# First MLP of a fused attention and two-MLP kernel: one visit of four units per token tile and group, later tile's h kept in the attention's buffers

## Chip, cores and metric

One core of a Trainium2 (trn2) chip. The metric is the device time of one execution in microseconds (us), as the median of several runs.

## What is computed

A block-summary attention (2 batches, 8 heads, 768 positions, head dimension 64), then two MLPs over its 1536 tokens of 512 channels, both with 2048 hidden units. The first MLP's activation is a rational function, the second's is h cos(h). All data are float32, the weights of the MLPs float64.

```python
def _attn_ref(q, k, v):
    block, window = (32, 16)
    k_sum = k.reshape(B, H, nb, block, D).max(axis=3)
    v_sum = v.reshape(B, H, nb, block, D).mean(axis=3)
    scores_l = scale * np.matmul(q, k.transpose(0, 1, 3, 2))
    scores_s = scale * np.einsum('bhsd,bhnd->bhsn', q, k_sum) + np.log(block)
    # softmax over |i - j| < 16 and the 24 block summaries, times v and v_sum

def _moe_ref(x, w_in, w_out, a, b):
    h = x @ w_in
    P = a[0] + a[1] * h + a[2] * h2 + a[3] * h3
    Q = 1.0 + np.abs(b[0]) * np.abs(h) + np.abs(b[1]) * h2
    return (P / (Q + 1e-06)) @ w_out

def _moe2_ref(x, w_in, w_out):
    h = x @ w_in
    return (h * np.cos(h)) @ w_out
```

## The kernel before

The instructions of all engines are recorded first by Python functions as operations with their reads and writes (`P.op`, where "T" is TensorE, "A" ScalarE, "V" VectorE, "P" GpSimd and "S" SyncE, whose queue issues the DMAs). A table of numbers, `ORDER`, then gives the sequence in which the operations are issued, and for each the engine where several are allowed (`Plan.order`). So the order on an engine isn't the order of the code.

*Attention.* Twelve query tiles u of 128 tokens. `attn_a` (L605 on) gathers the windows of k, multiplies q by them (tiles `sp`, L633), adds the mask and takes the minimum on VectorE (L663), the exponential with its row sum on ScalarE (L667), adds 1e-9 to the row sums (L672, L674), takes the reciprocal (L677) and scales (L680), the last three once for each of the two halves `hh` of the heads. `attn_b` transposes (L694), `attn_c` multiplies by v (`avp`, L741) and writes x transposed in two parts, high and low (`xH`, `xL`), since every product is done as three float32r matmuls: high by high, high by low, low by high. A query tile also needs the k tiles and the means of v (`k_pair`, `k_tile`, `v_mean0`, `v_mean1`).

*MLPs.* The tokens are three tiles T of 512. The hidden units are 16 slices f of 128, in four groups of four (`G = 4`). A unit is a pair (T, f): `mlp_h` (L909) makes h in a PSUM bank from 12 matmuls, the activation (`ew1` or, for Strassen pairs, `ew1s`) makes g and splits it into `gh` and `gl`, and `mlp_o` (L1307) multiplies g by the output weights into four PSUM accumulators, acc0 to acc3 (12 matmuls, L1341). The outputs of a unit come three units after its h (`LA = 3`). The accumulators hold one token tile at a time. A stretch of consecutive units of one T is called a visit here. At its end the accumulators are copied out to a partial sum in SBUF (`part` for T = 0 and 1, `room` for T = 2), or, after the last slice, kept as the next MLP's x (`x_keep`). At the start of a later visit they are copied back into PSUM (the `if un.first and have` branch of `mlp_o`). All of these copies are 128 x 512, on ScalarE or VectorE.

In the first group tile 0 is done in two halves of 256 columns (c = 0 and 256), so that it can begin when two of its four query tiles are done. In the later groups tiles 0 and 1 are a Strassen pair: `mlp_h4` (L1087) makes the h of two slices f, f + 1 and both tiles by seven products of six matmuls (L1111) instead of eight. Its parts h11, h12, h21, h22 are copied out of, or added to, three PSUM banks (`keep`, `plus`, L1119 to L1124) into four tiles of the pool `t`, where they wait for their activation. `sum_pair` (L819) makes the four sums of weights that the products need (S1 to S4, high and low), for every second pair in a buffer of tag `big`, for the others in four buffers that the attention has left (tags `sc`, `sc`, `pt`, `qk`). `x_pair0` makes the sums of x. `conv` converts weights from float64 (three VectorE instructions, L767, L771, L775) and splits them (L784); `run_conv` says when.

The order of units in a later group, before: tile 2 stands alone, first or last; tile 1 is entered with two slices, then tile 0 with four, then tile 1 with two.

```python
    two = [(1, f0), (1, f0 + 1)] + [(0, f0 + i) for i in range(G)] + [(1, f0 + 2), (1, f0 + 3)]
    flat += [(T, f, 0, TT) for T, f in (single + two if g % 2 else two + single)]
```

In the second MLP tile 2 has a Strassen form of its own (`mlp_h2`, L1160) and its visits are as in the first. `mlp_end` (L1378) finishes the last accumulator of the last unit in two halves of 256 columns, each with its own copy and transfer.

## Times and profile before

| | us |
|---|---|
| median of 3 runs | 595.98 (595.64 to 599.79) |
| the profiled execution | 596.73 |
| its span, first to last instruction | 595.0 |
| TensorE matmul busy | 574.7 (97%) |
| VectorE busy | 540.3 (91%) |
| ScalarE busy | 449.2 (75%) |
| GpSimd busy | 351.8 (59%) |

PE is the matmul side of TensorE, PEld its weight loads, DVE VectorE, ACT ScalarE, POOL GpSimd, SPq SyncE's queue. A group of rows names the line of the kernel, the engine, the operation and its tiles as out<-in. "Idle before" is the time for which the engine had nothing to do just ahead of an instruction, with what ended it. PEclk is the granted TensorE clock as a share of full speed. Matmuls overlap in their pipeline: one of 512 columns takes some 390 ns, and the next begins 227 ns after it.

### The profile page before, as it was taken

To read this page: it belongs to the slowest core of one execution; us is meant where nothing else is said; L and a number is where in the kernel's file an instruction comes from. 1 tells how busy PE (TensorE), PEld (TensorE's weight loads), DVE (VectorE), ACT (ScalarE), POOL (GpSimd) and SP (SyncE) were. 2 spreads that over 40 slices of the span, in tenths; PEclk is the share of its full clock that TensorE was granted. 3 is DMA by queue.
4 is the path that set the end of the run, shared out by engine and by line. 5 is a ranking of instruction groups with operands and counts; after the bars stand their busy time and mean duration, and the time that the engine had idled before them with its cause. 6 is when DMAs were issued, how large, how long until landed. Compare 5 with 4: busy or idle time off the path is not lost.

```text
span 595.0 us, 10350 instructions
## 1 busy us (share of the span) xinstructions
PE 574.7 (97%) x3567; PEld 477.0 (80%) x3567; DVE 540.3 (91%) x1101; ACT 449.2 (75%) x980; POOL 351.8 (59%) x342
## 2 busy tenths in 40 slices
PE   7969999999999999999999899999999999999997
PEld 6568787888888787888778678888889888888886
DVE  4999999999999999999899999998997898897773
ACT  3989999989799999999799996856446234555452
POOL 5768978767879677777777606354444415344031
PEclk9999999999999999999999999999999999999999
DMA  8996941301122131312122221113322132020013
GB/s 243 284 257 168 254 100 42 98 21 56 67 73 69 37 106 36 105 51 93 36 71 72 72 72 36 43 64 106 107 71 72 36 103 75 1 72 0 2 72 141
DMA packets 68861, 51.83 MB, mean 87 GB/s; under 512 B 37304, under 2 KB 63160, under 8 KB 68808
## 3 DMA queue, kind: packets, MB, share of 16 engines
q1 hardware_dynamic: 68664, 51.03, 29.1%
q8 instruction: 28, 0.46, 0.3%
q14 instruction: 25, 0.20, 0.1%
q10 hardware_dynamic: 144, 0.13, 0.1%
HBM read 47.71 MB, written 3.15 MB: 85 GB/s over the span
## 4 chain that ended last, share of the span: by engine, by line
PE 56%; ACT 21%; DVE 15%; issue 3%; POOL 2%; DMA 2%; SPq 1%; DVEq 0%; ACTq 0%; POOLq 0%
PE acc L1341 26%; PE h L1111 12%; PE h L924 7%; PE h L1160 6%; ACT acc L328 2%; ACT tt L1211 2%; ACT h L1215 2%; ACT h L1229 2%; DVE f L775 1%; PE ptp L694 1%; ACT gh L328 1%; ACT tf L1213 1%; PE avp L741 1%; ACT part L328 1%; DVE sc L663 1%
## 5 line engine op out<-in xcount | busy, mean ns | idle before, releaser
L1341 PE MATMUL acc<-gh,w 128*128 128x512 f32 (+1 forms) x416 | 123.3, 379 | 2.7 <-ACT acc L328 2.7
L1341 PE MATMUL acc<-w,gh 128*128 128x512 f32 x382 | 118.1, 391 | 0.0
L784 POOL TENSOR_TENSOR gl<-tt,gh 128x512 fp32r<-128x512 f32 (+1 forms) x59 | 75.6, 1284 | 53.1 <-ACT gh L328 34.5
L1341 PEld LDWEIGHTS acc<-gh,w 128*128 128x128 f32 x416 | 75.2, 188 | 19.0 <-ACT acc L328 4.8
L1341 PEld LDWEIGHTS acc<-w,gh 128*128 128x128 f32 x382 | 70.5, 188 | 14.0 <-ACT part L322 0.4
L784 POOL TENSOR_TENSOR w<-f,w 128x512 fp32r<-128x512 f32 x44 | 60.1, 1369 | 30.8 <-DVE w L333 23.3
L1341 PE MATMUL acc<-gl,w 128*128 128x512 f32 (+1 forms) x208 | 77.7, 373 | 0.0
L1341 PE MATMUL acc<-w,gl 128*128 128x512 f32 x191 | 74.4, 390 | 0.0
L328 ACT COPY tt<-h 128x512 f32<-128x512 f32 (+1 forms) x66 | 35.2, 538 | 30.3 <-PE h L1111 19.3
L924 PE MATMUL h<-big,w 128*128 128x512 f32 x216 | 53.0, 389 | 0.0
L1298 ACT ACTIVATE h<-h 128x512 f32<-128x512 f32 x48 | 27.3, 579 | 30.0 <-DVE h L1295 29.8
L924 PEld LDWEIGHTS h<-big,w 128*128 128x128 f32 x216 | 40.5, 188 | 8.5
L1292 ACT ACTIVATE h<-tt 128x512 int32<-128x512 f32 x48 | 28.6, 602 | 24.6 <-DVE tt L1124 8.6
L771 DVE SCALAR_TENSOR_TENSOR f<-raw,f 128x512 int32<-128x512 int32 x64 | 46.5, 729 | 0.4
L775 DVE SCALAR_TENSOR_TENSOR f<-raw,f 128x512 int32<-128x512 int32 x64 | 46.1, 728 | 0.3
L1341 PEld LDWEIGHTS acc<-gl,w 128*128 128x128 f32 x208 | 39.1, 188 | 7.0
L1295 DVE SCALAR_TENSOR_TENSOR h<-h,tt 128x512 f32<-128x512 int32 x48 | 32.9, 694 | 10.3 <-ACT h L1292 10.2
L1341 PEld LDWEIGHTS acc<-w,gl 128*128 128x128 f32 x191 | 35.9, 188 | 7.6
L1111 PE MATMUL h<-xH,w 128*128 128x512 f32 x120 | 41.7, 390 | 0.0
L328 ACT COPY part<-acc 128x512 f32<-128x512 f32 x50 | 29.0, 591 | 12.7 <-PE acc L1341 12.6
L1220 POOL TENSOR_TENSOR tt<-tt,tf 128x512 f32<-128x512 f32 x21 | 29.3, 1396 | 15.4 <-ACT tt L1211 10.5
L667 ACT ACTIVATE sc<-sc,mn 128x120 f32<-128x120 f32 x96 | 37.3, 392 | 0.0
(267 smaller groups left out, 1593.0 us busy)
## 6 DMA issues: line engine op xcount, KB each, us to landing
raw<-in_moe_w_in_dram SPq DMA_DIRECT2D x32, 512.0 KB, 4.1
raw<-in_moe_w_out_dram SPq DMA_DIRECT2D x32, 512.0 KB, 3.4
vw<-in_v_dram SPq DMA_DIRECT2D x24, 192.0 KB, 4.0
qk<-in_q_dram SPq DMA_DIRECT2D x10, 256.0 KB, 4.3
out_dram<-part SPq DMA_DIRECT2D x8, 256.0 KB, 2.4
part<-in_k_dram SPq DMA_DIRECT2D x8, 192.0 KB, 6.0
big<-in_v_dram SPq DMA_DIRECT2D x3, 512.0 KB, 6.8
qk<-in_k_dram SPq DMA_DIRECT2D x6, 256.0 KB, 4.8
```

The lines of the kernel that those rows point to most:

```text
L328: nc.scalar.copy(out=o, in_=i)
L667: lambda e, pr=pr, hh=hh, sv=sv: nc.scalar.activation(out=sv()[:, pr, :], in_=sv()[:, pr, :], func=ACTF.Exp, scale=-1.0, bias=mn.t[:, hh, ...
L771: lambda e: nc.vector.scalar_tensor_tensor(out=ft.t.bitcast(I32), in0=lohi()[1], scalar=-0x40000000, in1=ft.t.bitcast(I32), op0=ALU.bitwis ...
L775: lambda e: nc.vector.scalar_tensor_tensor(out=ft.t.bitcast(I32), in0=lohi()[0], scalar=29, in1=ft.t.bitcast(I32), op0=ALU.logical_shift_r ...
L784: lambda e: E[e].tensor_tensor(out=lo(), in0=x(), in1=hi().bitcast(F32), op=ALU.subtract),
L924: nc.tensor.matmul(out=h.t[:, 0:n], lhsT=lt, rhs=rt[:, kk, cs], start=(k0 == 0 and i == 0), stop=(k0 == 2 and i == 5))
L1111: nc.tensor.matmul(out=bank.t, lhsT=lt, rhs=rt, start=start and i == 0, stop=stop and i == 5, skip_group_check=True)
L1160: nc.tensor.matmul(out=bank.t[:, c], lhsT=lt, rhs=rt, start=start and i == 0, stop=stop and i == 5, skip_group_check=True)
L1220: lambda e: E[e].tensor_tensor(out=U(), in0=U(), in1=Z(), op=ALU.add))
L1292: lambda e: nc.scalar.activation(out=H().bitcast(I32), in_=S_(), func=ACTF.Identity, scale=1.0 / PER, bias=0.25))
L1295: lambda e: nc.vector.scalar_tensor_tensor(out=H(), in0=H().bitcast(I32), scalar=-PER, in1=S_(), op0=ALU.mult, op1=ALU.add))
L1341: nc.tensor.matmul(out=dst, lhsT=lt, rhs=rt, start=(un.start and not have and i == 0), stop=(un.stop and i == 2), skip_group_check=have)
```

## The change

- The first group does only slices 0 and 1 of tile 0 in halves; slices 2 and 3 are whole.
- In each later group of the first MLP tiles 0 and 1 are visited once each, with four units, tile 0 first in odd groups and tile 1 first in even ones. So tile 1 of group 1 is followed by tile 1 of group 2 without a break.
- `mlp_h4` keeps the two h tiles of the later tile of each pair in the attention's buffers (`sc`, `sc` for the first pair of a group, `pt`, `qk` for the second).
- `sum_pair` therefore puts all its sums into the `big` buffer, the two pairs of a group in its two halves, and `run_conv` holds back a pair's conversion until the pair four slices earlier has been multiplied (`made4`).
- In the attention, from query tile 2 on, the two halves' row sums get one add and one reciprocal together.
- `mlp_end` does the last accumulator's matmuls in whole width; the copies and transfers stay halves.
- `ORDER` is another table. The matmuls' `start` flags follow the new units.

```diff
--- before.py
+++ after.py
@@ -54,54 +54,53 @@
 
 
 ORDER = (
-    "c-rk)OOGVSagL14dcWV@UEN*%n0`#ZXNEJgyED79yIhjH;*ydnT9gQ
...
+    "c-rk*OOG5!a*mA1toOUBtGcSIr(e@O(=*K(a%RMbNQsXnceRu#P~=h
...
 )
 
 
@@ -667,20 +666,23 @@
                      lambda e, pr=pr, hh=hh, sv=sv: nc.scalar.activation(
                          out=sv()[:, pr, :], in_=sv()[:, pr, :], func=ACTF.Exp, scale=-1.0,
                          bias=mn.t[:, hh, pr:pr + 1], accum_out=su.t[:, hh, pr:pr + 1]))
-            sus = [su[hh, pr] for pr in range(NP)]
+            scs.append((sv, [sc[pr] for pr in range(NP)]))
+        for hs in ([0], [1]) if u < 2 else ([0, 1],):
+            sus = [su[hh, pr] for hh in hs for pr in range(NP)]
+            sl = slice(hs[0], hs[-1] + 1)
             P.op([("A", 0.11), ("V", Shared(0.08))], [], sus,
-                 lambda e, hh=hh: (nc.scalar.activation(out=su.t[:, hh], in_=su.t[:, hh],
+                 lambda e, sl=sl: (nc.scalar.activation(out=su.t[:, sl], in_=su.t[:, sl],
                                                         func=ACTF.Identity, bias=1e-9) if e == "A" else
-                                   nc.vector.tensor_scalar(out=su.t[:, hh], in0=su.t[:, hh], scalar1=1e-9,
+                                   nc.vector.tensor_scalar(out=su.t[:, sl], in0=su.t[:, sl], scalar1=1e-9,
                                                            scalar2=None, op0=ALU.add)))
             P.op([("V", 0.09)], [], sus,
-                 lambda e, hh=hh: nc.vector.reciprocal(out=su.t[:, hh], in_=su.t[:, hh]))
-            ss = [sc[pr] for pr in range(NP)]
-            P.op([("P", Shared(0.95)), ("V", dve2(480))], sus, ss,
+                 lambda e, sl=sl: nc.vector.reciprocal(out=su.t[:, sl], in_=su.t[:, sl]))
+        for hh in range(2):
+            sv, ss = scs[hh]
+            P.op([("P", Shared(0.95)), ("V", dve2(480))], [su[hh, pr] for pr in range(NP)], ss,
                  lambda e, hh=hh, sv=sv: E[e].tensor_tensor(
                      out=sv(), in0=sv(), in1=su.t[:, hh].unsqueeze(2).to_broadcast([128, NP, KW]),
                      op=ALU.mult))
-            scs.append((sv, ss))
         pr_t[u] = scs
         P.now += SPT
 
@@ -827,16 +829,10 @@
                   lambda w=w: w.t[:, 1, :], prio)
             made0[f + i] = w
             ws.append(w)
-        if f % 4 == 0:
-            if not spare2:
-                spare2.append(new("big", [128, 8, 512], F32R, "big", 2))
-            bt = spare2[0]
-            four = [(bt[i], lambda i=i: bt.t[:, i]) for i in range(f % 8, f % 8 + 4)]
-        else:
-            four = []
-            for tag, nb in (("sc", 4), ("sc", 4), ("pt", 3), ("qk", 3)):
-                r = new("qk" if tag == "qk" else "at", [128, 512], F32R, tag, nb)
-                four.append((r, lambda r=r: r.t))
+        if not spare2:
+            spare2.append(new("big", [128, 8, 512], F32R, "big", 2))
+        bt = spare2[0]
+        four = [(bt[i], lambda i=i: bt.t[:, i]) for i in range(2 * f % 8, 2 * f % 8 + 4)]
         A, B = slice(0, 256), slice(256, 512)
 
         def add(o, i0, i1, op, reads, writes):
@@ -1093,7 +1089,11 @@
         for i in range(2):
             for T in range(2):
                 un = u[i, T]
-                un.s = tmp("te")
+                if l == 0 and T != first:
+                    pn, tag, nb = (("at", "sc", 4), ("at", "sc", 4), ("at", "pt", 3), ("qk", "qk", 3))[f % 4 + i]
+                    un.s = new(pn, [128, 512], F32, tag, nb)
+                else:
+                    un.s = tmp("te")
                 un.s2 = [un.s]
                 un.h = (bc if T else bb) if i == 0 or T != first else ba
                 un.hb = [un.h]
@@ -1341,7 +1341,7 @@
                     nc.tensor.matmul(out=dst, lhsT=lt, rhs=rt,
                                      start=(un.start and not have and i == 0),
                                      stop=(un.stop and i == 2),
-                                     skip_group_check=have)
+                                     skip_group_check=have or un.l == 0)
 
             if un.first and have:
 
@@ -1377,40 +1377,38 @@
 
     def mlp_end(un, w, ac, res, pr):
 
+        def mm(e):
+            gh, gl = un.gh.t[:, 384:512], un.gl.t[:, 384:512]
+            for i, (lt, rt) in enumerate(((gh, w.t[:, 0]), (gh, w.t[:, 1]), (gl, w.t[:, 0]))):
+                nc.tensor.matmul(out=ac.t, lhsT=lt, rhs=rt, start=False, stop=i == 2,
+                                 skip_group_check=True)
+
+        P.op([("T", 3 * MM)], [w["h"], w["l"], un.gh, un.gl], [ac], mm)
+        P.now += 3 * MM
         for x, (e0, q) in enumerate((("A", nc.scalar), ("V", nc.sync))):
             c = slice(256 * x, 256 * x + 256)
-
-            def mm(e, c=c):
-                gh, gl = un.gh.t[:, 384:512], un.gl.t[:, 384:512]
-                for i, (lt, rt) in enumerate(((gh, w.t[:, 0, c]), (gh, w.t[:, 1, c]), (gl, w.t[:, 0, c]))):
-                    nc.tensor.matmul(out=ac.t[:, c], lhsT=lt, rhs=rt, start=False, stop=i == 2,
-                                     skip_group_check=True)
-
-            P.op([("T", 0.35)], [w["h"], w["l"], un.gh, un.gl], [ac], mm)
-            P.now += 0.35
-            sl = (lambda c=c: pr.t[:, 3, c]) if un.T < 2 or un.l else (lambda c=c: pr.t[:, 0, 3, c])
             P.op([(e0, 0.3)], [ac], [res[x]],
-                 lambda e, c=c, sl=sl: cps(e, sl(), ac.t[:, c], 1.0 / TURN))
+                 lambda e, c=c: cps(e, pr.t[:, 3, c], ac.t[:, c], 1.0 / TURN))
             r0 = TT * un.T + 384
             P.op([("S", 0.4)], [res[x]], [],
-                 lambda e, c=c, sl=sl, q=q, r0=r0: q.dma_start(out=out[r0:r0 + 128, c], in_=sl()))
+                 lambda e, c=c, q=q, r0=r0: q.dma_start(out=out[r0:r0 + 128, c], in_=pr.t[:, 3, c]))
 
 
     units = []
-    flat = [(0, f, c, 256) for c in (0, 256) for f in range(G)]
+    flat = [(0, f, c, 256) for c in (0, 256) for f in range(2)] + [(0, f, 0, TT) for f in range(2, G)]
     flat += [(T, f, 0, TT) for T in (1, 2) for f in range(G)]
     for g in range(1, NF // G):
         f0 = G * g
         single = [(2, f0 + i) for i in range(G)]
-        two = [(1, f0), (1, f0 + 1)] + [(0, f0 + i) for i in range(G)] + [(1, f0 + 2), (1, f0 + 3)]
+        two = [(T, f0 + i) for T in ((0, 1) if g % 2 else (1, 0)) for i in range(G)]
         flat += [(T, f, 0, TT) for T, f in (single + two if g % 2 else two + single)]
     for i, (T, f, c, n) in enumerate(flat):
         un = Unit()
         un.l, un.f, un.T, un.c, un.n = 0, f, T, c, n
         un.first = i == 0 or flat[i - 1][0] != T
-        un.start = un.first or (f == 0 and c > 0)
+        un.start = un.first
         un.spill = i + 1 == len(flat) or flat[i + 1][0] != T
-        un.stop = un.spill or (f == G - 1 and n < TT)
+        un.stop = un.spill
         un.last = un.spill and f == NF - 1
         units.append(un)
 
@@ -1494,8 +1492,12 @@
         last_use[un.l, un.f] = i
     WB = G + 1
 
+    made4 = set()
+
     def run_conv(i, prio):
         while state["c"] < len(conv_order) and (
+                conv_order[state["c"]] not in {(0, f) for f in range(2 * G, NF, 2)}
+                or (0, conv_order[state["c"]][1] - G) in made4) and (
                 state["c"] < G or i >= G and (state["c"] < WB or last_use[conv_order[state["c"] - WB]] <= i)):
             conv(*conv_order[state["c"]], prio)
             state["c"] += 1
@@ -1515,7 +1517,6 @@
     run_conv(-1, P.now)
     run_fill(pos_need[0])
     n = len(units)
-    made4 = set()
     for s in range(n + LA):
         if s < n:
             run_fill(pos_need[s])
```

Counts from the order: 96 matmuls of 256 columns in the first MLP become 48 of 512 (and 96 remain), reciprocals 24 become 14, copies of 128 x 512 on ACT 182 become 159, casts of that size 127 become 143; on DVE those casts go from 31 to 23, on GpSimd the copies and casts from 48 to 42.

ACT at the last re-entry of the first MLP, before (`part_2239` is tile 1's partial sum, `part_4252` is tile 0's x for the second MLP, acc0 to acc3 the accumulators):

```order
L328 COPY acc1_4263<-part_2239 128x512
L322 ACTIVATE part_4252<-acc0_4191 128x512
L1229 ACTIVATE h_4034<-tf_4233 128x512
L1292 ACTIVATE h_4166<-tt_4237 128x512
L328 CAST w1_4279<-f_4188 128x512
L322 ACTIVATE part_4252<-acc3_4126 128x512
L328 COPY acc0_4288<-part_2239 128x512
L1298 ACT_TABLE_LOAD
L1298 ACTIVATE h_4166<-h_4166 128x512
L322 ACTIVATE part_4252<-acc2_4118 128x512
L328 COPY acc3_4306<-part_2239 128x512
L328 CAST gh_4328<-tt_4074 128x512
L328 COPY acc2_4332<-part_2239 128x512
```

ACT at the same place in the change (`part_2151` is tile 1's partial sum, `part_4055` tile 0's x; the fourth copy back, of acc0, stands ten rows further on, still ahead of the table load):

```order
L327 CAST gh_4050<-sc_3683 128x512
L321 ACTIVATE part_4055<-acc2_3906 128x512
L321 ACTIVATE part_4055<-acc3_3899 128x512
L327 COPY acc2_4062<-part_2151 128x512
L321 ACTIVATE part_4055<-acc1_3869 128x512
L327 COPY acc3_4070<-part_2151 128x512
L327 CAST w0_4076<-f_4059 128x512
L327 COPY acc1_4084<-part_2151 128x512
L1229 ACTIVATE h_3875<-tf_3993 128x512
```

Before, the table load and the activation after it stand between the second and the third copy back; in the change they come after all four.

PE at that place, before (the accumulators change their number where the visit changes; `h_4143` is tile 2's next h, `h_4310` a second-MLP product):

```order
L1341 MATMUL acc3_4126<-gh_4235,w1_3901 128x512 x2
L1341 MATMUL acc3_4126<-gl_4239,w1_3901 128x512
L1341 MATMUL acc2_4118<-gh_4235,w1_3901 128x512 x2
L1341 MATMUL acc2_4118<-gl_4239,w1_3901 128x512
L1341 MATMUL acc1_4263<-gh_4249,w1_3822 128x512 x2
L1341 MATMUL acc1_4263<-gl_4260,w1_3822 128x512
L924 MATMUL h_4143<-big_1789,w0_4050 128x512 x6
L1341 MATMUL acc0_4288<-gh_4249,w1_3822 128x512 x2
L1341 MATMUL acc0_4288<-gl_4260,w1_3822 128x512
L1160 MATMUL h_4310<-big_1789,qk_4257 128x256 x2
L1160 MATMUL h_4310<-big_1789,pt_4308 128x256
```

PE at that place in the change (`h_4012` and `h_4115` are h of tile 2 in the second MLP):

```order
L1341 MATMUL acc1_3869<-gh_4023,w1_3779 128x512 x2
L1341 MATMUL acc1_3869<-gl_4028,w1_3779 128x512
L920 MATMUL h_4012<-big_1723,w0_3698 128x512 x6
L1341 MATMUL acc0_3937<-gh_4023,w1_3779 128x512 x2
L1341 MATMUL acc0_3937<-gl_4028,w1_3779 128x512
L1341 MATMUL acc2_4062<-gh_4050,w1_3382 128x512 x2
L1341 MATMUL acc2_4062<-gl_4072,w1_3382 128x512
L1341 MATMUL acc1_4084<-gh_4050,w1_3382 128x512 x2
L1341 MATMUL acc1_4084<-gl_4072,w1_3382 128x512
L1341 MATMUL acc3_4070<-gh_4050,w1_3382 128x512 x2
L1341 MATMUL acc3_4070<-gl_4072,w1_3382 128x512
L920 MATMUL h_4115<-big_1723,w0_4076 128x512 x12
```

Before, one returned accumulator, acc1, comes right after the old visit's last group (acc2), then half an h and the next returned one, acc0; in the change three returned accumulators follow each other after the old visit's last group (acc0), and an h of twelve matmuls comes after them.

SyncE's first DMAs, before (`part` takes k, `cb` a constant, `raw` a weight):

```order
L461 DMA part_174<-in_k_dram 128x2x192
L388 DMA cb_105<-in_moe_b_dram 128x2
L461 DMA part_189<-in_k_dram 128x2x192
L461 DMA part_174<-in_k_dram 128x2x192 x2
L422 DMA raw_203<-in_moe_w_in_dram 128x4x128
L461 DMA part_174<-in_k_dram 128x2x192
L461 DMA part_189<-in_k_dram 128x2x192 x2
```

SyncE's first DMAs in the change:

```order
L387 DMA cb_105<-in_moe_b_dram 128x2
L421 DMA raw_178<-in_moe_w_out_dram 128x512
L460 DMA part_186<-in_k_dram 128x2x192 x2
L460 DMA part_209<-in_k_dram 128x2x192 x4
L460 DMA part_186<-in_k_dram 128x2x192
L565 DMA part_186<-in_q_dram 128x4x128
L565 DMA part_209<-in_q_dram 128x4x128
```

The constant and a weight of 512 KB are now issued ahead of all k; before, a weight came after four k loads. The second piece of q also moved ahead of the last k.

## Rows read from the trace of the kernel before

**Rows 1.** The page: busy time by engine, and shares of the chain.

```profile
PE 574.7 (97%) x3567; PEld 477.0 (80%) x3567; DVE 540.3 (91%) x1101; ACT 449.2 (75%) x980; POOL 351.8 (59%) x342
...
PE 56%; ACT 21%; DVE 15%; issue 3%; POOL 2%; DMA 2%; SPq 1%; DVEq 0%; ACTq 0%; POOLq 0%
```

**Rows 2.** Busy us by stretch: length, PE, PEld, DVE, ACT, POOL, PEclk, DMA, GB/s.

```profile
0.00:20.00 20.00, 16.13 (x246) 12.93 (x247) 11.90 (x58) 10.63 (x42) 12.22 (x38) 1.00 0.90 260
20.00:116.00 96.00, 87.63 (x1125) 72.64 (x1123) 92.16 (x318) 89.55 (x307) 76.12 (x80) 1.00 0.66 170
116.00:180.00 64.00, 64.00 (x284) 53.03 (x283) 63.12 (x104) 56.40 (x98) 47.06 (x36) 1.00 0.18 56
180.00:360.00 180.00, 175.75 (x779) 142.39 (x778) 174.13 (x286) 170.39 (x307) 124.33 (x104) 1.00 0.21 66
360.00:580.00 220.00, 219.84 (x1090) 186.71 (x1089) 193.21 (x330) 118.33 (x223) 90.22 (x85) 1.00 0.18 58
580.00:595.00 15.00, 11.30 (x53) 9.28 (x51) 5.80 (x10) 3.92 (x8) 1.88 (x2) 1.00 0.37 140
```

**Rows 3.** What weight loads waited for, 180 to 360 us: total, times, longest.

```profile
PEld acc L1341 <- ACT acc L328: 4.8, 6, 1.4
PEld h L1111 <- ACT tt L328: 2.5, 4, 1.5
PEld h L1111 <- POOL qk L784: 0.7, 1, 0.7
...
PEld h L1111 <- POOL sc L784: 0.3, 1, 0.3
```

**Rows 4.** Timeline, end of first MLP: start, us, instruction, idle before it.

```profile
339.94 0.73 PE L1341 MATMUL acc<-gh,w 128*128 128x512 f32 x2 [0.32 <-ACT acc L328]
...
342.17 0.61 ACT L328 COPY acc<-part 128x512 f32<-128x512 f32 x1
...
342.83 0.73 PE L1341 MATMUL acc<-gh,w 128*128 128x512 f32 x2 [1.22 <-ACT acc L328]
```

**Rows 5.** Groups by line: count, busy us, mean ns, idle before.

```profile
L328 ACT CAST gh<-tt 128x512 fp32r<-128x512 f32 x51 | 31.8, 623 | 4.0 <-PE acc L1341 1.6 <-DVE tt L1301 1.4 <-DVE tt L1278 0.5
L328 ACT COPY acc<-part 128x512 f32<-128x512 f32 x54 | 31.5, 593 | 1.0 <-DVE part L333 0.9
...
L1278 DVE SCALAR_TENSOR_TENSOR tt<-tt,co,h 128x512 f32<-128x512 f32 x20 | 14.9, 744 | 0.3
...
L333 DVE CAST gh<-tt 128x512 fp32r<-128x512 f32 x19 | 9.4, 494 | 1.9 <-PE acc L1341 1.5
...
L677 DVE RECIPROCAL su<-su 128x4 f32<-128x4 f32 x24 | 4.0, 171 | 0.1
...
L1278 DVE SCALAR_TENSOR_TENSOR tt<-tt,co,h 128x256 f32<-128x256 f32 x8 | 3.8, 478 | 0.1
```

**Rows 6.** The chain in order of time, head to 120 us: start, us, what.

```profile
3.29 0.47 SPq L422
...
4.35 5.98 DMA part<-in_k_dram
...
31.52 1.43 PE h L924 x12
...
118.31 4.08 PE h L924 x18
```

**Rows 7.** Timeline of PE in the head: start, us, instruction, idle before it.

```profile
7.38 1.53 PE L470 MATMUL ktp<-ident,part 128*64 128x128 f32 x24 [0.83 <-DMA part<-in_k_dram]
10.47 2.19 PE L470 MATMUL ktp<-ident,part 128*64 128x128 f32 x36 [1.56 <-DMA part<-in_k_dram]
```

**Rows 8.** Timeline, tail: the last copy, and the issue of its transfer.

```profile
591.41 0.42 DVE L324 TENSOR_SCALAR room<-acc 128x256 f32<-128x256 f32 x1 [4.19 <-PE acc L1386]
592.04 0.38 SPq L1396 DMA_DIRECT2D out_dram<-room  x1
```

95 lines of the change are left out of this document (47 added, 48 removed).

## The prediction

> **What bounds the kernel now.** I read the engines' totals first. The span is 595.0 us; TensorE (PE) is busy for 574.7 of it and VectorE (DVE) for 540.3, and the chain that ended last runs 56% on PE, 21% on ScalarE (ACT) and 15% on DVE [rows 1]. A share over the whole span hides stages, so I cut it by what the kernel does [rows 2]. In the head (0 to 20 us) PE is busy 16.1 of 20.0 us and DVE 11.9, and the DMA engines are 90% busy: the inputs set the pace. In the attention (20 to 116 us) DVE is busy for 92.2 of 96.0 us and PE for 87.6: DVE sets the pace. From 116 to 180 us PE never stops. From 180 to 360 us, the groups of the first MLP that the change rewrites, PE is idle for 180.0 - 175.75 = 4.25 us, with DVE (174.1) and ACT (170.4) nearly full. From 360 to 580 us, the second MLP, PE is idle for 0.16 us; nothing can be won there except by removing matmuls. After 580 us there is a tail of 15 us with 11.3 us of PE.
>
> So the time can fall in three places only: the head, the attention, and those 4.25 us. For the last I read what the weight loads, PE's first step for a matmul, waited for in that stretch: 4.8 us in six waits for ACT writing an accumulator (a partial sum copied back into PSUM at the start of a visit) and 2.5 us in four for ACT copying an h product out [rows 3]. The sum over weight loads is larger than PE's idle time because a load can wait while the matmul ahead of it still runs; 4.25 is what PE lost. The timeline shows the shape at the end of the first MLP: ACT copies back at 342.17, and the matmul that needs it starts at 342.83 after 1.22 us without work; at 339.94 it was 0.32 us [rows 4].
>
> **The change, part by part.** Times are for the profiled execution: 596.73 us, of which 595.0 are the span. It stands 0.75 us above the median of the runs, 595.98.
>
> *Visits.* A visit is a stretch in which one token tile holds the four accumulators. Counting the list of units, 12 visits in the first MLP become 9, since tile 1 is no longer entered twice around tile 0 in each group. A visit that isn't a tile's last ends with four copies out, one that isn't its first begins with four back; 36 + 36 copies become 24 + 24. At 0.593 us for such a copy on ACT [rows 5], 24 x 0.593 = 14.2 us leave ACT and DVE. PE gets of this only what it waited for. If just the three visits' share of the nine re-entries goes, 3/9 x 4.8 = 1.6 us; if every wait goes, 4.25. The order decides between them. ACT's rows for the last re-entry of the first MLP show a gain: before, the four copies back are spread among a table load and two casts; now they come before the table load, with one further on. But ACT is not emptied: by the order it takes 16 casts of 512 columns more than before (0.623 us each, 10.0 us), which DVE (8, 0.494 us each) and GpSimd gave up [rows 5]. Of the 24 copies 23 go from ACT, 13.6 us, so its net relief is 3.6 us; DVE's is 4.0. DVE stays nearly full in this stretch. I take half of the 4.8, 2.4 us, and keep 1.6 and 4.25 as the ends.
>
> *Held h.* Both Strassen pairs of a group are now computed in its first two-tile visit, and the later tile's four h tiles stay in the attention's buffers. The seven products per pair, and the seven copies or adds after them, are as many as before. What is late next is here: in the later visit PE has 4 x 12 output matmuls of 0.227 us (18 of the same width take 4.08 us [rows 6]), 10.9 us, while DVE has five instructions per unit as long as the one of 744 ns [rows 5], 4 x 5 x 0.744 = 14.9 us. The difference, 4.0 us per group, is hidden if products of the next group stand between, which the order has for two of three groups (tile 2's, or tile 1's next pairs); for the last, products of the second MLP. I take 0; without the cover it costs 4.0 per group, up to 12.0 for three.
>
> *The S sums.* Every pair's weight sums now use one 8-part buffer alternately, and a pair's sums wait until the pair four f earlier has been multiplied. Behind such a wait stand, on DVE and GpSimd, the conversions of the next weights, and PE behind those. In the trace the weight loads wait twice for such operands, 0.7 and 0.3 us [rows 3]. Cost between -1.0 (these waits go) and +1.0 (as much comes again); I take 0.
>
> *Softmax.* For ten of twelve query tiles the two sets of row sums share one add and one reciprocal. DVE loses ten reciprocals at 0.171 us [rows 5], 1.7 us, and four adds, which I price alike at 0.7. Each merged instruction now waits for eight exponentials rather than four, and the first half's scaling with it; the scaling is on GpSimd, not full in this stretch (76.1 of 96.0 us [rows 2]).
>
> *Half units.* For tile 0 only f = 0 and 1 are still done in halves of 256 columns. On DVE, five instructions per unit fall from four halves to two wholes: 4 x 0.478 - 2 x 0.744 = 0.42 us for the longest [rows 5], at most 2.1 us for five. On PE, 12 half matmuls take 1.43 us where six whole ones take 1.36 [rows 6]; eight such dozens leave, so 8 x 0.07 = 0.56 us, of which only what falls after the attention counts; I take 0.3.
>
> The two give DVE 4.5 us at most in a stretch that it sets. But its order now does more of other work before the last attention instruction (casts of weights, sums of x for the first pair), which takes the place of some. Ends 0 and 4.5 us; I take 2.0.
>
> *Head.* SyncE now issues one constant and a 512 KB weight ahead of the k loads, where before one k load led and a weight came after four. An issue of a weight takes 0.47 us [rows 6], so k starts about 0.9 us later, and the piece of k that ended the head's longest wait (5.98 us, landing at 10.33 [rows 6]) has the same bytes ahead of it. Against this, the weight's conversion, three DVE instructions, fills time in which DVE is idle, 8.1 us of the first 20. Ends +1.5 and -1.5; I take 0.
>
> *End.* The last accumulator gets three whole matmuls instead of six halves. The half that ends last is sent at 592.04 [rows 8]; it still follows the last matmul. ACT's half loses a head start that nobody needed. Zero, within 0.4 either way.
>
> The sum: -2.4 - 2.0 - 0.3 = -4.7 us, so 592.0 for a profiled execution and **591.3 us** for the median. A measurement of this kernel can tell about 1%, 6 us, from no change; the forecast lies inside that.
>
> **The clock.** The granted clock was 1.00, the upper level of 2.4 GHz, in every stretch [rows 2], although PE stood still for 0.83 and then 1.56 us among the k transposes [rows 7]. The Trainium skill ("TensorE: Matmul & The Clock Gate", part 1 on the clock gate) says that the array's clock halves after idleness and comes back only after sustained work. By that rule the later k loads would be dearer than I count; the trace has no such drop, so it is a rival and not a term.
>
> **Rivals.**
> *A. All of it arrives.* Attention -4.5, PE's idle -4.25, -0.3: 595.98 - 9.05 = 586.9 us. For it: DVE is full in the attention, so what it loses is time; the order was made for the new work. Against: DVE is given other work there.
> *B. DVE takes it back.* The copies that go stood mostly on ACT; DVE, full to 174.1 of 180 us, remains the engine for which PE waits. Then 1.6 us from the visits and none from the attention: 594.4. For it: the waits for h copies and weights remain.
> *C. Slower: the later visit starves.* The 4.0 us per group is not covered, PE stands in each later visit waiting for gh and gl, 12.0 us: 591.3 + 12.0 = 603.3. It makes the kernel slower by 1% as soon as PE's idle time in those groups grows from the 1.85 us that I leave to 1.85 + 4.7 + 6.0 = 12.6 us. Against: nearly 11 us of other products per group can stand there.
> *D. The clock falls in the head.* With k late, PE runs at the lower level until it has worked for a while; its longest piece among the k transposes, 2.19 us [rows 7], doubles: 591.3 + 2.2 = 593.5 us. The bound above is all its 16.1 us of the head.
> *E. The change does not hold four h apart*, because the buffers are still in use by the first pair's operands. Then the products wait for x sums in turn, like B.
>
> **How the numbers follow.** Forecast 0.41, A 0.27, B with E 0.21, C 0.08, D 0.03. Below 590.0 us lie A and about a third of the forecast's own spread (588 to 595): 0.27 + 0.13 = 0.40. Above 602 lies C: 0.08. The rest is 0.52. The range goes from 586.5, just under A's value, to 597.5, B with 3 us of head and weights lost; it leaves out C, part of A and part of D.
>
> **What would show it.** Right: the rows of copies between accumulators and partial sums lose 24; PE's waits for ACT's accumulator copies fall to about 2.4 us; the last attention matmul ends near 114 us instead of 116; PE's idle time between 180 us and the second MLP is near 2 us; the second MLP and the tail are as long as before. Wrong: new waits of the output matmuls for gh or gl in the later tile's visit (C); a granted clock under 1.00 in the head (D); DVE's idle time unchanged and PE's too (B).

## The result, and the profile after

The changed kernel takes 603.68 us (median of 6 runs, 602.32 to 605.15) against 595.97 us for the kernel before, run beside it on the same chip: a ratio of 1.0117, 95% interval 1.0092 to 1.0143. It is slower by about 7.7 us, where 4.7 less were forecast; the time lies above the range. The profiled execution took 602.32 us (span 600.6), that of before 596.73 (span 595.0).

The page of the changed kernel, busy time by engine and shares of the chain, answers to [rows 1]:

```profile
PE 575.6 (96%) x3516; PEld 472.8 (79%) x3516; DVE 540.9 (90%) x1064; ACT 443.9 (74%) x955; POOL 344.4 (57%) x334
...
PE 52%; DVE 23%; ACT 12%; issue 5%; POOL 4%; DMA 2%; SPq 1%; ACTq 0%; DVEq 0%; POOLq 0%
```

DVE went from 15% to 23% of the chain and ACT from 21% to 12%: the copies on ACT are off it, and VectorE has come in. The same stretches as in [rows 2] without the first and the last (length, PE, PEld, DVE, ACT, POOL, PEclk, DMA, GB/s):

```profile
...
20.00:116.00 96.00, 87.49 (x1061) 69.37 (x1054) 88.59 (x303) 88.74 (x294) 74.43 (x72) 1.00 0.65 164
116.00:180.00 64.00, 62.60 (x279) 50.22 (x275) 63.43 (x100) 51.98 (x92) 43.40 (x34) 1.00 0.19 58
180.00:360.00 180.00, 174.90 (x775) 140.90 (x774) 174.81 (x283) 161.72 (x287) 130.20 (x108) 1.00 0.20 62
360.00:580.00 220.00, 219.92 (x1080) 186.47 (x1079) 190.87 (x314) 123.25 (x233) 83.04 (x81) 1.00 0.19 59
```

PE's idle time rose from 0 to 1.40 us between 116 and 180 and from 4.25 to 5.10 between 180 and 360. DVE's busy time in the attention fell from 92.2 to 88.6 of 96 us, and PE did no more work there for it. What the weight loads waited for from 180 to 360 us (total, times, longest) answers to [rows 3]:

```profile
PEld h L1111 <- ACT pt L327: 2.4, 1, 2.4
PEld acc L1341 <- ACT acc L327: 1.2, 2, 0.8
PEld h L1111 <- ACT tt L327: 1.1, 1, 1.1
PEld h L1111 <- ACT qk L327: 1.1, 1, 1.1
PEld h L1111 <- DVE tt L1278: 1.0, 1, 1.0
PEld acc L1341 <- POOL gl L786: 0.9, 1, 0.9
PEld h L1111 <- DVE qk L1124: 0.9, 2, 0.6
```

The waits for accumulators copied back fell from 4.8 to 1.2 us, more than was counted on. In their place the seven products wait for a copy, an addition or a last read that frees their bank. The later tile's visit does not starve for gh or gl (one wait of 0.9).

The tail is longer too. Here are its last copies, and ACT's issue of its transfer, which took 0.37 us before:

```profile
594.41 0.39 PE L1383 MATMUL acc<-w,gl 128*128 128x512 f32 x1
594.84 0.42 DVE L323 TENSOR_SCALAR room<-acc 128x256 f32<-128x256 f32 x1 [0.67 <-PE acc L1383]
595.36 0.38 ACT L321 ACTIVATE room<-acc 128x256 f32<-128x256 f32 x1 [1.96 <-DVE room L323]
...
595.77 2.37 ACTq L1394 DMA_DIRECT2D out_dram<-room  x1
```

To see where the loss lies in each kernel, I took from the traces the start of the last attention matmul (avp), the end of the last matmul, and the end of the span (us; "half rate" is told of below):

| | last avp | last matmul | between | tail | median of runs |
|---|---|---|---|---|---|
| before | 115.8 | 591.3 | 475.5 | 3.7 | 595.97 |
| after | 116.0 | 594.8 | 478.8 | 5.8 | 603.68 |
| e1, halved end | 114.5 | 593.3 | 478.8 | 5.1 | 601.28 |
| e2, before with the whole end | 115.8 | 591.3 | 475.5 | 3.7 | 595.95 |
| e3, product copies earlier | 117.9 (half rate) | 597.0 | 479.0 | 5.9 | 603.57 |
| e4, ten DVE instructions exchanged | 114.2 | 588.7 | 474.5 | 5.9 | 597.05 |
| e5, e4 and SyncE's queue | 116.5 (half rate) | 590.9 | 474.4 | 4.3 | 595.92 |
| e10, e5 and one more exchange | 120.3 (half rate) | 594.7 | 474.4 | 4.2 | 597.07 |
| e11, e5 and 20 reciprocals | 117.2 | 591.6 | 474.4 | 4.2 | 599.77 |
| e12, e5 and a longer warm-up | 114.2 | 588.6 | 474.3 | 4.5 | 595.20 |
| e6, after's structure, new order | 116.2 (half rate) | 590.3 | 474.1 | 4.3 | 596.00 |
| e7, before's structure, new order | 115.3 | 588.8 | 473.4 | 4.7 | 595.16 |

The stretch between the last avp and the last matmul hardly differs between executions of one order (478.8 to 479.0 with after's, 474.4 to 474.5 with that of e4), so it is the best measure here. Of the 5.6 us by which the two profiled executions differ, 3.3 lie in it, 2.1 in the tail and 0.2 ahead.

The 0.2 us ahead hide three larger parts. The first avp starts 1.1 us later than before (27.2 against 26.1). The products from first to last start would be 2.5 us shorter, as in e1, whose attention is that of after (87.2 against 89.7). But in after's execution they were only 0.9 shorter, since one of them waited for a transfer of v. Up to there e1, e4 and after run alike; the transfer was issued at 70.7 to 70.8 us in each and took 7.3 us in after, 5.8 in e1 and 5.7 in e4. The products in after, then the wait in after and in e1:

```profile
L743 PE MATMUL avp<-pt,vw x384: 222/222/271, 27.2 to 116.0; 120*64 120x64 f32 x192
...
78.17 1.24 PE L743 MATMUL avp<-pt,vw 120*64 120x64 f32 x32 [1.98 <-DMA vw<-in_v_dram]
...
76.70 1.16 PE L741 MATMUL avp<-pt,vw 120*64 120x64 f32 x32 [0.47 <-DMA vw<-in_v_dram]
```

So 1.5 us of what a run gains against after's profiled execution ahead of the last avp can be this transfer and no effect of its edit.

### The profile page after: what moved, and what is told of

The parts are those of the page before. It is cut to its first block, busy times and chain, and to the rows that moved or that the text cites. A ratio compares the mean times of both kernels' runs of the same rounds, so it can differ in the third digit from the quotient of the medians.

```text
span 600.6 us, 10128 instructions
## 1 busy us (share of the span) xinstructions
PE 575.6 (96%) x3516; PEld 472.8 (79%) x3516; DVE 540.9 (90%) x1064; ACT 443.9 (74%) x955; POOL 344.4 (57%) x334
## 4 chain that ended last, share of the span: by engine, by line
PE 52%; DVE 23%; ACT 12%; issue 5%; POOL 4%; DMA 2%; SPq 1%; ACTq 0%; DVEq 0%; POOLq 0%
PE acc L1341 25%; PE h L1111 12%; PE h L1160 6%; PE h L920 4%; DVE f L773 2%; DVE tt L1272 2%; DVE h L1275 2%; DVE f L777 2%; DVE tt L1262 2%; DVE tt L1264 2%; DVE tt L1278 2%; DVE f L769 1%; ACT h L1229 1%; ACT h L1215 1%; DMA vw<-in_v_dram 1%
## 5 line engine op out<-in xcount | busy, mean ns | idle before, releaser
L1341 PE MATMUL acc<-gh,w 128*128 128x512 f32 (+1 forms) x400 | 121.1, 385 | 0.5 <-ACT acc L327 0.4
L786 POOL TENSOR_TENSOR gl<-tt,gh 128x512 fp32r<-128x512 f32 (+1 forms) x50 | 67.0, 1343 | 47.7 <-ACT gh L327 34.2
L786 POOL TENSOR_TENSOR w<-f,w 128x512 fp32r<-128x512 f32 x47 | 64.9, 1383 | 49.1 <-ACT w L327 39.7
L1341 PEld LDWEIGHTS acc<-gh,w 128*128 128x128 f32 x400 | 73.3, 188 | 15.4 <-ACT acc L327 1.2
L1341 PE MATMUL acc<-gl,w 128*128 128x512 f32 (+1 forms) x200 | 76.3, 382 | 0.5 <-POOL gl L786 0.5
L327 ACT COPY tt<-h 128x512 f32<-128x512 f32 (+1 forms) x57 | 29.7, 523 | 29.6 <-PE h L1111 12.3
L777 DVE SCALAR_TENSOR_TENSOR f<-raw,f 128x512 int32<-128x512 int32 x64 | 51.0, 800 | 0.4
L773 DVE SCALAR_TENSOR_TENSOR f<-raw,f 128x512 int32<-128x512 int32 x64 | 46.6, 733 | 0.4
L1341 PEld LDWEIGHTS acc<-gl,w 128*128 128x128 f32 x200 | 37.5, 188 | 8.4 <-POOL gl L786 0.9
L327 ACT CAST gh<-tt 128x512 fp32r<-128x512 f32 (+1 forms) x53 | 32.6, 615 | 14.0 <-PE acc L1341 7.3
L1301 DVE TENSOR_TENSOR tt<-tt,h 128x512 f32<-128x512 f32 x48 | 32.4, 681 | 8.1 <-ACT h L1298 7.7
```

The lines of the kernel that those rows point to most:

```text
L327: nc.scalar.copy(out=o, in_=i)
L773: lambda e: nc.vector.scalar_tensor_tensor(out=ft.t.bitcast(I32), in0=lohi()[1], scalar=-0x40000000, in1=ft.t.bitcast(I32), op0=ALU.bitwis ...
L777: lambda e: nc.vector.scalar_tensor_tensor(out=ft.t.bitcast(I32), in0=lohi()[0], scalar=29, in1=ft.t.bitcast(I32), op0=ALU.logical_shift_r ...
L786: lambda e: E[e].tensor_tensor(out=lo(), in0=x(), in1=hi().bitcast(F32), op=ALU.subtract),
L1301: lambda e: E[e].tensor_tensor(out=S_(), in0=S_(), in1=H(), op=ALU.mult))
L1341: nc.tensor.matmul(out=dst, lhsT=lt, rhs=rt, start=(un.start and not have and i == 0), stop=(un.stop and i == 2), skip_group_check=have or ...
```

## The experiments

Theories: T1, the whole-width end and the order of its copies cost the tail 2 us. T2, the products' copies stand behind other work on ACT and DVE. T3, VectorE and GpSimd block each other, since the new order sets instructions of the two that touch SBUF only side by side. T3 comes from this place of the changed kernel (start, us, instruction, idle before it):

```profile
312.08 0.69 DVE L1222 TENSOR_TENSOR h<-h,tt 128x512 f32<-128x512 f32 x1
312.68 1.79 DVE L777 SCALAR_TENSOR_TENSOR f<-raw,f 128x512 int32<-128x512 int32 x1
314.39 0.74 DVE L1224 SCALAR_TENSOR_TENSOR tt<-h,co,tt 128x512 f32<-128x512 f32 x1
...
312.63 1.29 POOL L786 TENSOR_TENSOR big<-room,big 128x512 fp32r<-128x512 f32 x1
...
315.22 0.60 ACT L1229 ACTIVATE h<-tf 128x512 f32<-128x512 f32 x1 [0.89 <-DVE tt L1224]
315.76 0.58 ACT L327 COPY pt<-h 128x512 f32<-128x512 f32 x1
...
316.39 0.97 PE L1111 MATMUL h<-qT,big 128*128 128x512 f32 x3 [1.97 <-ACT pt L327]
```

GpSimd's subtraction began 0.05 us ahead of DVE's weight conversion and held it up until 0.55 us after its own end: 1.79 us instead of 0.69. DVE's next instruction was late, so ACT's, so the copy behind it, and PE stood for 1.97 us. Between 95 and 360 us the trace of after has 12 DVE instructions that took over 0.3 us longer than the median of their line and shape, 9.6 us in sum; that of before has 7, 3.4 us. Each of the 12 ran beside a GpSimd instruction and ended 0.53 to 0.55 us after it, or 0.28 us after it for the four that usually take 0.42 us, three of which (the first step of the weight conversion, L769) have one operand only.

**e1 and e2: the end.** In e1 the changed kernel gets before's halved end, in e2 the kernel before gets the whole-width end:

```diff
-        P.op([("T", 3 * MM)], [w["h"], w["l"], un.gh, un.gl], [ac], mm)
...
         for x, (e0, q) in enumerate((("A", nc.scalar), ("V", nc.sync))):
             c = slice(256 * x, 256 * x + 256)
...
+            P.op([("T", 0.35)], [w["h"], w["l"], un.gh, un.gl], [ac], mm)
```

> The changed kernel with the last output tile cut in two halves again, as before the change: two groups of three matmuls over 256 columns, the left half first, eleven matmuls groups ahead of the right one, its copy on ScalarE and its transfer under the products that are left. Theory T1 (the end): in the changed kernel the tail from the last matmul to the end of the span took 5.8 us against 3.7, because ScalarE's copy of its half waited 1.96 us for VectorE's copy of the other half of the same bank and its transfer was issued last, with 2.37 us. T1 expects the tail back at 3.6 to 4.0 us and the time 1.8 to 2.3 us under the changed kernel, so 601.4 to 601.9. The rivals (waits of products for their banks, collisions of VectorE and GpSimd) expect the last matmul where it is, at 594.8 us of the span, since nothing ahead of the last unit is touched. If all of the loss were at the end, the time would come to about 596.

> The kernel before the change with only the end of the changed one: one group of three matmuls over 512 columns, VectorE's half copied and sent first, then ScalarE's. T1 expects the tail from 3.7 to 5.5 to 6.0 us and the time 1.8 to 2.3 us above before, at 597.8 to 598.3; everything ahead of the last unit unchanged. If the end costs nothing (as the prediction had it), the time stays within 0.4 us of before.

e1: 601.28 us, ratio to before 1.0068 (1.0045 to 1.0091); ACT's issue still took 2.33 us. e2: 595.95, ratio 0.9984 (0.9965 to 1.0004), and its issue took 0.37 us although its end is whole. T1 falls: the whole end itself costs nothing, and with the halved end the tail went from 5.8 to 5.1 us only. That e1's time lies near the 601.4 to 601.9 of T1 is luck: in its profiled execution 1.5 of the 2.2 us are the transfer of v above. What the slow issues have and e2's has not is that meanwhile a DMA queue brings instructions (the DMA queues of after from 593 us on; no instruction queue moved anything at the end of before or of e2):

```profile
q1 hardware_dynamic: 720, 1.18, 40.8%
q14 instruction: 1, 0.01, 0.6%
```

**e3 and e4: the order.** e3 moves one product copy of ACT (at 159.4 us) and one sum of DVE (163.0) two places ahead. e4 sets ten SBUF-only DVE instructions that had collided one or two places later, eight of them behind an instruction that reads h in PSUM; at 312 us:

```diff
 L1222 TENSOR_TENSOR h<-h,tt
-L777 SCALAR_TENSOR_TENSOR f<-raw,f
 L1224 SCALAR_TENSOR_TENSOR tt<-h,co,tt
+L777 SCALAR_TENSOR_TENSOR f<-raw,f
```

> The changed kernel with two evacuations of Strassen product banks moved two places up, nothing else: ScalarE's copy of c22 at 159.4 us of the traced run, and VectorE's sum into c11 at 163.0 us. Theory T2 (the copies of product banks stand behind activations on engines that work in order, so that the gain of the longer visits comes back as waits of the products): the waits of PE for its product banks between 155 and 180 us, 2.0 us in the changed kernel, fall by 1.0 to 1.5, and the time by about as much, to 602.2 to 602.7. Theory T3 (which of VectorE and GpSimd has the shared port first is decided by some 0.1 us, so that any shift reshuffles the collisions behind it): the end moves by more than the waits that were taken away, up or down, by up to 4 us, and the VectorE instructions that run over 0.95 us inside a GpSimd one stand at other places from 160 us on.

> The changed kernel with ten VectorE instructions that read and write SBUF alone, and stood still inside a GpSimd instruction in the trace (at 105.0, 123.1, 154.9, 161.0, 167.3, 255.1, 276.7, 281.5, 289.5 and 312.7 us), moved one or two places down on VectorE, behind instructions with a PSUM operand, which no GpSimd instruction holds up. No wait and no instruction is added. T3: the long stalls at those places go, VectorE's excess over its median durations in the first 360 us falls from 12.1 us to 9 or less, and the last matmul ends 1 to 4 us earlier: 599.5 to 602.5. T2: nothing is gained, since the copies of product banks stand where they stood: 603 to 604. New collisions behind the first shift can eat a part of the gain under T3.

e3: 603.57 us, ratio 1.0104 (1.0070 to 1.0139), as after. The move did not take the wait away: the product behind it stood for 1.95 us at 169.8 us, where it stood for 0.89 in after, and then the granted clock was 0.50 from 171.2 to 174.6 us. Both together put e3 2.5 us further behind after, and by 213 us it had made up 2.4 of them, so a stop of PE there is not by itself what sets the time behind it. That speaks against T2 for these two copies; others were not moved.

e4: 597.05 us, ratio 1.0006 (0.9987 to 1.0025): by the medians the ten exchanges take away 6.6 of the 7.7 us. By the traces 4.6 are theirs: the stretch behind the attention falls from 478.8 to 474.5, and the last avp starts 0.3 us earlier than in e1 (1.8 earlier than in after, 1.6 of it the transfer of v). Of the 9.6 us of lengthened DVE instructions 3.6 are left. The lead of e4's matmuls over after's grows from 1.9 us at 111 us to 4.1 at 175, behind four of the ten places, and to 6.2 at 316, behind the last. The same place in e4:

```profile
306.89 0.69 DVE L1220 TENSOR_TENSOR h<-h,tt 128x512 f32<-128x512 f32 x1
307.68 0.75 DVE L1222 SCALAR_TENSOR_TENSOR tt<-h,co,tt 128x512 f32<-128x512 f32 x1
308.35 1.53 DVE L775 SCALAR_TENSOR_TENSOR f<-raw,f 128x512 int32<-128x512 int32 x2
...
307.44 1.29 POOL L784 TENSOR_TENSOR big<-room,big 128x512 fp32r<-128x512 f32 x1
...
310.20 0.96 PE L1109 MATMUL h<-qT,big 128*128 128x512 f32 x3 [0.90 <-ACT pt L325]
```

The instruction that reads h in PSUM takes its usual 0.75 us inside GpSimd's, the conversion behind it loses a quarter of a microsecond, and PE stands for 0.90 instead of 1.97 us. So it is shown that the order of these ten instructions made most of the loss behind the attention, and that DVE instructions are held up there. How much of it the holding up made is not: the exchange also sets the read of h ahead by the length of the instruction that it passes, 0.69 of the 1.79 us here, collision or not, and no run has the exchange without the collision. That part of T3 is argued, and T2 is not excluded for those reads.

**e5 and e10: the transfer, and one more exchange.** e5 is e4 with ACT's half of the end sent from SyncE's queue; e10 exchanges one more pair of DVE instructions of e5.

```diff
-        for x, (e0, q) in enumerate((("A", nc.scalar), ("V", nc.sync))):
+        for x, (e0, q) in enumerate((("A", nc.sync), ("V", nc.sync))):
```

> The kernel with the ten VectorE swaps, and the transfer of ScalarE's half of the last tile issued on SP's queue instead of ScalarE's; nothing else. In the runs so far ScalarE's one transfer took 2.37 us to issue in the changed kernel, 2.33 with the split end and 2.53 with the swaps, and an 8 KB instruction fetch lies inside each of the three; in the kernel before, and in that kernel with the whole end, it took 0.37 and no fetch lies there. If the fetch is what the end lost (T1, as now understood), the tail falls from 5.9 to 3.7 to 4.1 us and the time by 1.8 to 2.2, to 595.0 (594.4 to 595.6). If it is the order of the two copies from one bank, the tail stays over 5.5 us and the time at 597.

> e5 with one more pair of VectorE instructions exchanged: the sum of two SBUF tiles that began at 178.83 us inside a GpSimd difference and took 1.79 us now stands behind the next instruction, which reads PSUM. T3: the next instruction no longer waits 1.1 us, 595.9 - 0.5 to 1.1 = 594.8 to 595.4; the trace shows the read of PSUM at its usual 0.69 us ahead of the sum. If the collision is not what delays PE: unchanged, 595.9.

e5: 595.92 us, ratio 0.9997 (0.9977 to 1.0017), tail 4.3 us instead of 5.9. e10: 597.07, ratio 1.0013 (0.9993 to 1.0033); the stretch behind the attention stayed at 474.4. That exchange gained nothing: one collision became two smaller ones.

**e6 and e7: structure or order.** Behind 112 us the order was made anew by the same rules for both structures; `ORDER` is the only edit, to e5 and to the kernel before.

> The changed kernel with both of its transfers of the end on SyncE, and with a new order from the last query tiles (about 112 us) on; 86 operations also change their engine. It is to be read beside e7, where the kernel before has its order made anew in the same stretch by the same rules. T3 (the changed kernel lost its gain to the order of VectorE and GpSimd, not to its structure): under e5's 595.9, at 590 to 594, since its visits keep their gain of 1.6 to 4.25 us once nothing collides. T4 (the structure itself is worth nothing, since what PE waited for at the copies it now waits for elsewhere): within 1 us of e5, 595 to 597.

> The kernel before with a new order from the last query tiles (about 112 us) on, made by the same rules as that of e6; 153 operations also change their engine. T3 and the prediction's term for the visits: slower than e6 by the 1.6 to 4.25 us of three visits, so 593 to 597. T4 (the structure is worth nothing; a good order brings either kernel to the same time): within 1 us of e6.

e6: 596.00 us, ratio 0.9992 (0.9973 to 1.0012). e7: 595.16, ratio 0.9978 (0.9955 to 1.0001). The two can't be told apart, and behind the attention the old structure is 0.7 us shorter (473.4 against 474.1). The order made the loss: e6 has after's structure, and its stretch is 4.7 us shorter than after's. With these two orders the structure makes no gain, as T4 says. That it can make none is not shown, since e6's order still has 13 DVE instructions that took over 0.3 us longer than their median between 95 and 360 us, 8.4 us in sum, where e7's has 6, 2.9 us. The same count shows that the sum is no price: after has 9.6 us of it and 478.8 us, e6 8.4 and 474.1. Windows and weight-load waits from 180 to 360 us, of e6 and then of e7:

```profile
180.00:360.00 180.00, 177.70 (x789) 143.60 (x788) 177.88 (x289) 163.26 (x290) 133.40 (x110) 1.00 0.20 64
```

```profile
PEld h L1108 <- DVE tt L1234: 1.4, 2, 1.2
PEld h L1108 <- DVE qk L1121: 1.0, 1, 1.0
PEld acc L1338 <- ACT acc L324: 1.0, 3, 0.4
PEld h L1157 <- DVE tt L329: 0.9, 1, 0.9
```

```profile
180.00:360.00 180.00, 177.46 (x790) 143.82 (x789) 176.13 (x289) 170.34 (x305) 123.16 (x105) 1.00 0.22 68
```

```profile
PEld acc L1337 <- ACT acc L324: 3.7, 5, 1.4
PEld h L1107 <- ACT tt L324: 1.1, 2, 0.6
```

e7 waits 3.7 us for the copies back, e6 1.0; e6 waits instead for DVE, which is busy for 177.9 of 180 us there. PE works equally long in both.

**e11: is DVE's time in the attention worth anything?**

```diff
-                 lambda e, sl=sl: nc.vector.reciprocal(out=su.t[:, sl], in_=su.t[:, sl]))
+                 lambda e, sl=sl: [nc.vector.reciprocal(out=su.t[:, sl], in_=su.t[:, sl])
+                                   for _ in range(1 if u < 2 else 3)][-1])
```

> e5 with the reciprocal of the row sums done three times (the value is the same) for the ten query tiles with merged row sums: 20 more VectorE instructions of 0.19 us, 3.8 us, in the attention. The prediction's term (VectorE sets the attention's pace, what it loses or gets is time): +2 to +3.8 us, 598 to 599.7. T5 (the attention now waits for transfers and copies, VectorE's relief there was worth nothing, and its price is nothing too): within 1 us of 595.9.

599.77 us, ratio 1.0046 (1.0026 to 1.0066); e5's was 0.9997. The 3.8 us of DVE cost 2.9 (1.2 to 4.6 by the two intervals). So the premise holds and T5 falls: what DVE loses in the attention is time, about three quarters of it (from a third to more than all of it by the interval). The attention's products (first to last start) show the gain of the change as well, 2.7 us in e4 against before, and the loss of e11, 2.9 us against e12, which like e11 has no lower clock there:

```profile
L741 PE MATMUL avp<-pt,vw x384: 221/222/272, 26.1 to 115.8; 120*64 120x64 f32 x192
...
L741 PE MATMUL avp<-pt,vw x384: 222/222/271, 27.2 to 114.2; 120*64 120x64 f32 x192
...
L742 PE MATMUL avp<-pt,vw x384: 222/222/271, 27.3 to 117.2; 120*64 120x64 f32 x192
```

(before, e4, e11). But the first avp comes 1.1 us later: that is lost in the head, which was priced at 0.

**e12 to e14: the head.** In four of the ten profiled executions with the changed head that had been made by then most of the first 48 k transposes went at half their rate. Here is e6's row, after's (a full-rate one), then that of e12, with the longer warm-up:

```profile
6.11 4.78 PE L466 MATMUL ktp<-ident,part 128*64 128x128 f32 x48 [0.90 <-DMA part<-in_k_dram]
```

```profile
6.14 2.84 PE L469 MATMUL ktp<-ident,part 128*64 128x128 f32 x48 [0.93 <-DMA part<-in_k_dram]
```

```profile
6.13 3.04 PE L467 MATMUL ktp<-ident,part 128*64 128x128 f32 x48
```

The edit, 10 for e5 (e12) and e6 (e13), 6 for the kernel before (e14):

```diff
-        for i in range(8):
+        for i in range(10):
             nc.tensor.matmul(out=wu[:, 0:128], lhsT=ident, rhs=ident, start=True, stop=True)
```

> e5 with ten matmuls in the warm-up ahead of the transposes of k instead of eight, so that PE works until about 6.1 us, when the later k of the changed order lands, and no longer stops for 0.9 us there. T6 (rival D, in some executions only: after that stop the k transposes go at twice their spacing for 4 us in four of the ten executions that were profiled with the changed head, which costs 1.9 us each time): no doubled spacing at 6 us, and the median falls from e5's 595.9 by the share of executions that had it, 0.4 x 1.9 = 0.8 us, to 594.6 to 595.5, with the runs closer together. T7 (the doubling has another cause than the stop): it comes as often, and the median stays at 595.9 or rises by the added matmuls.

> e6, whose profiled execution had the doubled spacing of the k transposes at 6 us, with ten matmuls in the warm-up. T6: the transposes of k at 0.11 us each, not 0.21, and the median falls from e6's 596.0 by 0.8 to 1.9 us, to 594.1 to 595.2. T7: 596.0, spacing 0.21 again.

> The kernel before with six matmuls in the warm-up instead of eight, so that PE stops for about 0.9 us ahead of its k transposes, as the changed kernel does. T6: some executions get the doubled spacing there, and the median rises by 0.4 x 1.9 = 0.8 us or more, to 596.5 to 598. T7: unchanged within 0.5 us of the kernel before.

e12: 595.20 us, ratio 0.9986 (0.9971 to 1.0002); its runs lie within 594.3 and 596.1, where e5's fell into two groups, 594.5 to 595.2 and 596.7 to 597.3; in its profile the first four transposes are still slow. e13: 595.73, ratio 1.0001 (0.9983 to 1.0019), with the first ten transposes still at half rate in the profile. e14: 596.12, ratio 1.0001 (0.9981 to 1.0022); k landed early in its profiled execution and no stop came ahead of the first transposes, so it did not make the case it was meant for. It shows in one execution, at another place, what T6 supposes: behind a stop of 2.26 us at 10.5 us, 36 transposes took 3.12 us instead of before's 2.19, and from 11.6 to 15.0 us the granted clock was 0.50. e12 points to T6; the three do not settle it. e12 and e7 are the shortest kernels of the study, and neither can be told from the kernel before.

**Three kernels with a small DVE write** of 0.07 us into a new 64-byte tile per partition, ahead of the other buffers, meant to shift the times and see whether the collisions change:

```diff
+    pad = const.tile([128, 16], F32, name="pad")
...
+                nc.vector.memset(pad, 0.0)
```

> The changed kernel with one more instruction: VectorE clears 16 columns of a tile that nothing reads, ahead of its instruction at 60.2 us of the traced run. It costs VectorE some 0.06 us, at a time when PE waits for it now and then, so the work done says at most 0.1 us. T3 (who gets the shared port first is decided by some tenths of a us) expects the collisions behind it to fall otherwise, and the time to move by more than 1 us in either direction: 597 to 607, other than 603.7 by over 1. T2 and T1 expect 603.6 to 603.9.

> As the last, but ahead of VectorE's instruction at 122.4 us, where VectorE is busy 99% of the time: 0.06 us more of work. T3: the time moves by more than 1 us in either direction, most likely down, since in the changed kernel's trace the lock fell badly at most of the close places: 598 to 605. T1 and T2: 603.6 to 603.9.

> The kernel before with the same cleared 16 columns, ahead of VectorE's instruction at 122.1 us. T3: the time moves by more than 1 us, most likely up, since in the trace of before the close places mostly fell well (excess of VectorE in the first 360 us 10.4 us against 14.2): 595 to 601. The rivals: within 0.3 us of before.

608.42 us, ratio 1.0209 (1.0172 to 1.0246); 607.30, ratio 1.0191 (1.0148 to 1.0233); 600.77 for the kernel before, ratio 1.0079 (1.0053 to 1.0106). All three are 3.6 to 4.8 us slower, and the delay stands ahead of the last avp (119.8 to 121.4 us). In the two with the write at 126 to 128 us it is there before the write, so the instruction does not make it; the new tile is the only other edit. Between 95 and 360 us the lengthened DVE instructions are nearly those without the write, only later (12, 13 and 8 of them against 12, 12 and 7). The form of T3 in these expectations, that a small shift reshuffles the collisions, is therefore not borne out; beyond that the experiment missed its aim.

## Why the prediction was wrong

*Visits, -2.4 taken.* The waits fell as told (4.8 to 1.2 us). The step that failed is the one from there to time, "PE gets of this only what it waited for": the wait went and PE's idle time from 180 to 360 us rose, from 4.25 to 5.10 us, since other waits took its place. The prediction had that as rival B, "DVE takes it back", with 0.21; e6 and e7 bear it out for their two orders (stretches of 474.1 and 473.4 us), and its 594.4 is near what the structure gives once the order is mended (e5, 595.92; e12, 595.20).

*The order, no term at all.* This is the step that made the kernel slower instead of faster. The prediction read from the new table where single instructions moved, and counted nothing for where it sets DVE's SBUF-only instructions, beside GpSimd's and ahead of the reads of h. e4 shows that this was the largest term, and of the other sign: ten exchanges are worth 4.6 us in the traces. How it divides between the holding up and the place is open.

*Held h, 0 taken.* Right: no starving. Rival C's time, 603.3, was near, and its mechanism was not there.

*S sums, 0 within 1.* No experiment took them alone; in after the weight loads of the seven products show no wait for a sum between 180 and 360 us, where there were 0.7 and 0.3 us before.

*Attention, -2.0 taken.* Right in size from first to last avp (2.5 in e1, 2.7 in e4), and DVE does set the pace (e11). It did not arrive: 1.1 us went in the head, and in after's profiled execution 1.5 us to the late transfer of v.

*Half units, -0.3 taken.* No run took them alone.

*Head, 0 within 1.5.* Mis-sized: the first k load was issued 0.9 us later (1.70 against 0.80), as the step said, and the first avp came 1.1 us later, so nothing stood against it. Where the transposes went at half rate they took 1.9 us more and the first avp came 1.6 us later still. That is near the price of rival D (2.2), in some executions, though its sign, a granted clock under 1.00, did not stand at those transposes. Neither is in after's profiled execution, the shortest of its six. The other five were 1.1 to 2.8 us longer and had a mean granted clock of 0.995 or 0.996 against its 0.999; a stretch of 3.4 us at 0.50, like e3's, is 0.003 of the span. Where theirs lay no trace shows.

*End, 0 within 0.4.* Mis-sized: 2.1 us. The edit is free (e2), but ACT's issue met an instruction fetch. In e5 the fetch is still there (at 592.4 us), and with the issue on SyncE's queue the tail is 4.3 us. Why the fetch comes there in the changed program was not tried.

## What to carry to other kernels

Before an order is changed, list the SBUF-only instructions on VectorE and GpSimd that will stand beside each other, and what stands behind them: here ten exchanges by one or two places were worth more than nine visits instead of twelve. A wait that a change removes may come back as another one; compare two structures only after each has an order of its own. A change is best read from a stretch that repeats between executions, here from the last attention matmul to the last matmul; ahead of it one late transfer was worth 1.5 us.
